# An attention block whose front part takes four score maxima and six projection products in turn, with the first rows of maxima written by VectorE

## The chip, the core and the metric

The kernel runs on one core of a Trainium2 chip. The engines that matter are TensorE (PE in the profile, its weight loads PEld), VectorE (DVE), ScalarE (ACT), GpSimd (POOL) and SyncE (SP), which issues nearly all the transfers. Each engine and each issuing queue works through its own list of instructions in the order in which the program gave them; between engines there are only semaphores. The metric is the device time of one execution in microseconds (us), median over the runs. Lower is better.

## The reference

One transformer block, 2048 rows of 512 numbers, float32. A modulation vector (six parts of 512) comes from a small product with `w_mod`. The first half is attention with 32 query heads of 16 numbers and one shared head of keys and values; the second half an MLP of width 1376.

```python
x = A_x
mod = (_silu(c) @ w_mod).reshape(c.shape[0], 6, 1, -1)
sa, ca, ga, sb, cb, gb = (mod[:, i] for i in range(6))
h = _layernorm(x) * (1 + ca) + sa
q = (h @ wq) in 32 heads of 16;  k = h @ wk;  v = h @ wv
p = softmax(q k^T / 4);  o = p v
x = x + ga * (o @ wo)
h = _layernorm(x) * (1 + cb) + sb
x = x + gb * (gelu(h @ w1 + b1) @ w2 + b2)
```

The softmax needs, for each of 32 x 2048 query rows, the largest of its 2048 scores before the exponentials.

## The kernel before

**Units.** The attention is cut into 64 units: 8 blocks of 256 query rows, each with 8 groups of four heads. For one unit the program does two things, far apart in time. First the maxima: 32 products `m` of 128 query rows against 512 keys (indices j, t, kc, s: s is one of two halves of the array's rows, so that an s=0 and an s=1 product run beside each other), each followed by one VectorE reduction over 512 scores (`Max.step`, L512 and L517). Then the exponentials: 8 steps, each with four products `e` (L617), four ScalarE exponentials (L621) and the products `acc` of the exponentials with the values (L638). The maxima run ahead of the exponentials by a lead that the loop holds with a table, `lead[u]`: `LEAD_0` counts groups of four maxima beyond unit 1 at the start, `LEAD` the same from unit 8 on, with a straight line between. `mp.done` is the number of maxima issued; in every pair of steps the loop issues as many as bring it to the goal.

**Placing the maxima.** When the 32 reductions of a unit are in, `put_max` reduces them over kc (`mm`), transposes the result (`turned`), copies it in four pieces into one row per score column (`mt`), splits it into a high part `mh` and a rest `ml`, and sends both by DMA into rows 48 and 49 of each half of the unit's query tile `qst`. The matching rows of the keys hold -1, so the products `e` come out with the maximum already taken off. No `e` of a unit can start before its four sends have landed. In the running loop the copies and the split are GpSimd's (L560, L133, L140) and the sends SyncE's (L555); they are asked for by `later(n, ...)`, n quarter-iterations after the reductions are complete, which fixes their place in each engine's list. Of unit 0 two of the four sends are issued by ScalarE.

**The front part.** Before the loop, an explicit list `SLOTS` interleaves the maxima of units 0 and 1 with the rest of the preparation: `"keys b"` is a group of three products of the key and value projection of row block b (twelve in all, `kps`), after the fourth group two ScalarE copies write the keys (`kv_out`, L401) and one the values (L402); `"low b"` is a VectorE subtraction that writes the low part of the keys (L407), `"k b"` its ScalarE copy; `"heads b"` a transposition group with modulation; `"q 1"` three products of the second query projection; `"v b"` a transposition of the values; `"rows"` a quarter of the late modulation rows (`modl`, L297); `"wq g"` the split of a weight block; `"load"` the six loads of unit 2's query tile (`load_q`, L483). A number in a slot is a count of maxima. `FIRST_MAX` says in which order: all of unit 0's are done after 48. The `m` products use a ring of three PSUM banks (tag `m`); the banks `e0` to `e2` (`ebank()`) serve the transpositions in the front and the products `e` in the loop.

**Products that nobody reads.** `keep_warm(n)` issues n full products whose result is unread, in four places, the last just ahead of the loop (`WARM[3]`).

**SyncE's list in the loop.** The same queue carries the loads of the next query tiles (`load_q`: six transfers, and two of `dz` from unit 4 on) and, in the first units, the sends of the query projections (`dq`), the loads and stores of the weights being prepared (`w1f`, `dw`), and for a short while the late modulation rows (`drm`, `ga`, `gb`, `sb`, `cb`).

Of the kernel before, what the change touches and what calls it, by code (L numbers as in the profile page):

```python
# [22 lines left out]
LEAD_0 = 6  # L23
FIRST_MAX = ((0, 0), (1, 0), (0, 1), (1, 1), (0, 2), (0, 3), (1, 2), (1, 3))
SLOTS = ((2, "keys 1", "keys 1"), (2, "keys 1", "keys 1"), (2, "low 1", "heads 2"), (2, "heads 2", "k 1"), (1, "warm"), (1, "heads 2"), (2, "heads 2", "v 0"),
# [19 lines left out]
WARM = (4, 16, 2, 5)  # L45
# [4 lines left out]
def raw(ap):  # L50
    return ap.bitcast(F32)
# [3 lines left out]
def adaln_mqa_mlp(  # L55
# [230 lines left out]
    def keep_warm(n, **place):  # L286

        for k in range(n):
            if k == 0 or not place:
                ps = psum.tile([P, BQ], F32, name=f"idle{len(idles)}", **(place or dict(tag="m", bufs=3)))  # L290
                idles.append(ps)
            nc.tensor.matmul(ps, wkH[:, 0, :], wkH.rearrange("p k n -> p (k n)"), start=True, stop=True)
# [98 lines left out]
    def kv_products(b):  # L391
        hH, hL = hts[b]
        kps[b] = psum.tile([P, BQ], F32, name=f"kps{b}", tag="x" if b == 3 else "v")
        return mm3(kps[b], [(wkH[:, k, :], wkL[:, k, :], hH[:, k, :], hL[:, k, :]) for k in range(KD)], 3)

    def kv_out(b):
        ps = kps[b]
        cols = slice(b * BQ, (b + 1) * BQ)
        vt = pro.tile([P, BQ], F32, name=f"vt{b}", tag="vt", bufs=2)
        for r in range(2):  # L400
            nc.scalar.copy(ks[64 * r:64 * r + 48, cols], ps[64 * r:64 * r + 48, :])  # L401
        nc.scalar.copy(vt[32:64, :], ps[32:64, :])  # L402
        vts[b] = vt

    def low_k(b):
        cols = slice(b * BQ, (b + 1) * BQ)
        nc.vector.tensor_tensor(out=ks[32:48, cols], in0=kps.pop(b)[32:48, :], in1=raw(ks[32:48, cols]), op=ALU.subtract)  # L407
# [128 lines left out]
    def put_max(u, mx):  # L536
# [13 lines left out]
        def send():  # L550
            for s in range(2):
                for r, src in ((48, mh), (49, ml)):
                    dst = qst[64 * s + r:64 * s + r + 1].rearrange("p j (t n) -> p (j t) n", n=P)
                    ring = nc.scalar if u == 0 and s else nc.sync
                    ring.dma_start(out=raw(dst), in_=raw(src[2 * T * s:2 * T * (s + 1), :].unsqueeze(1)))  # L555
            placed.add(u)
# [7 lines left out]
        def reduce():  # L564
            nc.vector.tensor_reduce(out=mm[:, :4 * T], in_=mx, axis=AX.X, op=ALU.max)
# [672 lines left out]

    def chunk(n):
# [5 lines left out]
    def k_products(b):  # L1245
        for _ in kv_products(b):
            pass
# [84 lines left out]
    run(keys(0))  # L1332
    low_k(0)
# [19 lines left out]
    for n, *names in SLOTS:  # L1353
        chunk(n)
        for name in names:
            next(work[name])
# [53 lines left out]
    keep_warm(WARM[3], tag="e2", bufs=1)  # L1410
# [172 lines left out]
```

## Time and profile before

| what | value |
|---|---|
| runs | 1558.17, 1556.62, 1556.4 us; median 1556.62 |
| the profiled execution's own time | 1555.99 us |
| its span, first to last instruction | 1554.1 us |
| granted TensorE clock | 1.00 throughout |
| busy: PE, DVE, ACT, POOL | 99%, 90%, 79%, 44% of the span |
| first `m` of the front part | 31.84 us |
| first `e` of the loop | 75.14 us |
| first `acc` of the loop | 78.88 us |

A busy PE is not PE at its peak: its instructions are pipelined and their ends are modelled, so two rows that follow each other are compared by their starts. A row such as "48.68 5.27 DVE ... x8" is eight instructions merged, from their first start to their last end. What stands in brackets is the idle time of the engine ahead of the row and who ended it.

### The profile page before, as it was taken

Reading aid. Unit: us, or ns where it says so; the run is one execution under the profiler, and the core shown is the slowest. Engines: PE = TensorE matmul, PEld = TensorE weight load, DVE = VectorE, ACT = ScalarE, POOL = GpSimd, SP = SyncE. Lnnn points to the kernel's source line nnn. Section 1 sums busy time; section 2 is a strip of 40 time slices with the busy share of each in tenths; the row PEclk is TensorE's granted clock in tenths of the full one; section 3 lists DMA queues with packets and bytes.
Section 4 is the critical chain, followed back from the end, with each engine's and each line's share of the span. In section 5 each row is a group of like instructions: output and inputs, shape, how many; then the busy total and the mean of one; then the engine's idle time right before and its main releaser. Section 6 shows DMA issues by size and latency. Waiting matters only on the chain.

```text
span 1554.1 us, 41556 instructions
## 1 busy us (share of the span) xinstructions
PE 1537.9 (99%) x16405; PEld 954.4 (61%) x16405; DVE 1398.3 (90%) x2488; ACT 1230.4 (79%) x2401; POOL 683.7 (44%) x1206
## 2 busy tenths in 40 slices
PE   7999999999999999999999999999999999999999
PEld 4455555567655665557655676556655676566658
DVE  7999999999999999999999999999999999999814
ACT  5577778788877887788877888788877888778874
POOL 5535432867422571246521563235711574046511
PEclk9999999999999999999999999999999999999999
DMA  7226412413030220303112120302212230203141
GB/s 240 102 89 199 151 57 81 130 51 97 18 105 26 72 68 28 103 19 109 33 51 79 56 87 16 111 26 88 68 30 73 60 101 25 87 28 99 48 150 48
DMA packets 84215, 120.85 MB, mean 78 GB/s; under 512 B 21342, under 2 KB 57438, under 8 KB 83764
## 3 DMA queue, kind: packets, MB, share of 16 engines
q1 hardware_dynamic: 84004, 118.18, 23.7%
q8 instruction: 130, 2.13, 0.6%
q14 instruction: 65, 0.53, 0.1%
q10 hardware_dynamic: 16, 0.00, 0.0%
HBM read 90.87 MB, written 26.74 MB: 76 GB/s over the span
## 4 chain that ended last, share of the span: by engine, by line
PE 86%; DVE 8%; issue 3%; POOL 2%; DMA 1%; ACT 0%; SPq 0%; POOLq 0%; DVEq 0%
PE acc L638 29%; PE m L512 23%; PE e L617 16%; PE w1ps L198 8%; DVE mx L517 6%; PE w2ps L198 2%; PE w2ps L188 2%; DMA xt<-in_A_x_dram 1%; PE w1ps L188 1%; PE wops L198 1%; PE tp L198 1%; PE qps L198 1%; PE kps L165 1%; DVE st L823 0%; DVE x L816 0%
## 5 line engine op out<-in xcount | busy, mean ns | idle before, releaser
L517 DVE TENSOR_REDUCE mx<-m 128x1 f32<-128x512 f32 x2048 | 1270.6, 682 | 86.6 <-PE m L512 65.1
L621 ACT ACTIVATE p<-e 128x512 f32<-128x512 f32 x2048 | 1098.8, 598 | 255.1 <-PE e L617 112.0
L512 PE MATMUL m<-ks,qst 64*128 64x512 f32 x2048 | 836.7, 429 | 2.0 <-DVE mx L517 0.6
L617 PE MATMUL e<-qst,ks 64*128 64x512 f32 x2048 | 740.2, 412 | 0.0
L638 PE MATMUL acc<-p,va 128*32 128x256 f32 x8192 | 548.0, 385 | 0.0
L512 PEld LDWEIGHTS m<-ks,qst 64*128 64x128 f32 x2048 | 368.2, 184 | 205.1 <-DVE mx L517 173.5
L617 PEld LDWEIGHTS e<-qst,ks 64*128 64x128 f32 x2048 | 359.6, 184 | 89.3 <-ACT p L621 62.5
L638 PEld LDWEIGHTS acc<-p,va 128*32 128x32 f32 x8192 | 214.0, 109 | 213.9 <-issue 110.9
L198 PE MATMUL w1ps<-h2H,w1t 64*128 64x256 f32 x1232 | 235.5, 287 | 0.0
L560 POOL TENSOR_SCALAR mt<-turned 8x32 f32<-8x32 f32 x256 | 53.1, 208 | 399.9 <-DVE turned L566 387.9
L198 PEld LDWEIGHTS w1ps<-h2H,w1t 64*128 64x128 f32 x1232 | 186.0, 185 | 28.9 <-DVE mx L517 14.8
L198 PE MATMUL w1ps<-h2L,w1t 64*128 64x256 f32 x616 | 169.3, 275 | 0.0
L198 PE MATMUL w2ps<-w2H,gH 64*128 64x512 f32 x274 | 120.3, 439 | 0.0
L198 PEld LDWEIGHTS w1ps<-h2L,w1t 64*128 64x128 f32 x616 | 114.1, 185 | 0.0
L198 PE MATMUL w2ps<-w2L,gH 64*128 64x512 f32 x274 | 107.5, 392 | 0.0
L198 PE MATMUL w2ps<-w2H,gL 64*128 64x512 f32 x274 | 106.9, 390 | 0.0
L975 POOL TENSOR_SCALAR tt<-tt 128x256 f32<-128x256 f32 x77 | 31.0, 402 | 131.5 <-ACT tt L974 96.5
L140 POOL TENSOR_TENSOR gL<-z,gH 128x256 fp32r<-128x256 f32 x77 | 57.0, 741 | 6.4
L976 POOL TENSOR_TENSOR tt<-tt,z 128x256 f32<-128x256 f32 x77 | 56.7, 736 | 6.4
L986 POOL TENSOR_TENSOR z<-tt,z 128x256 f32<-128x256 f32 x77 | 56.4, 732 | 6.0
L985 POOL TENSOR_TENSOR tt<-tt,z 128x256 f32<-128x256 f32 x77 | 56.5, 733 | 0.0
L198 PEld LDWEIGHTS w2ps<-w2H,gH 64*128 64x128 f32 x274 | 50.4, 184 | 6.7 <-DVE ot L1038 2.5
(193 smaller groups left out, 1503.5 us busy)
## 6 DMA issues: line engine op xcount, KB each, us to landing
w1t<-dw SPq DMA_DIRECT2D x82, 512.0 KB
qst<-dq SPq DMA_DIRECT2D x384, 32.0 KB
do<-oc SPq DMA_DIRECT2D x62, 128.0 KB
dw<-w1s SPq DMA_DIRECT2D x11, 512.0 KB
xt<-in_A_x_dram SPq DMA_DIRECT2D x4, 1024.0 KB
dq<-qH SPq DMA_DIRECT2D x16, 256.0 KB
dq<-qL SPq DMA_DIRECT2D x16, 256.0 KB
x<-in_A_x_dram SPq DMA_DIRECT2D x8, 512.0 KB
```

The lines of the kernel that those rows point to most:

```text
L140: eng_l.tensor_tensor(out=dst_l, in0=src, in1=raw(dst_h), op=ALU.subtract)
L188: nc.tensor.matmul(ps, a, b_, start=first_, stop=last_)
L198: ins = nc.tensor.matmul(ps, a[rows], b_[rows], start=first_ and s == 0, stop=last_ and s == 1)
L512: nc.tensor.matmul(m, qsts[u][rows, j, t * P:(t + 1) * P], ks[rows, kc * 512:(kc + 1) * 512], start=True, stop=True)
L517: nc.vector.tensor_reduce(out=self.mx[u][:, i, kc:kc + 1], in_=m, axis=AX.X, op=ALU.max)
L560: nc.gpsimd.tensor_scalar(out=mt[:, g:g + 32], in0=turned[g:g + 4 * T, :], scalar1=1.0, scalar2=0.0, op0=ALU.mult, op1=ALU.add)
L617: nc.tensor.matmul(e, ks[rows, kt * P:(kt + 1) * P], rhs, start=True, stop=True)
L621: ins = nc.scalar.activation(dst, e, AF.Exp, scale=0.25)
L638: ins = nc.tensor.matmul(accs[u][32 * cidx:32 * cidx + 32, :], va[:, kt, :], rhs, start=kt == 0, stop=kt == NKT - 1)
L976: nc.gpsimd.tensor_tensor(out=tt, in0=tt, in1=z, op=ALU.mult)
L985: nc.gpsimd.tensor_tensor(out=tt, in0=tt, in1=z, op=ALU.mult)
L986: nc.gpsimd.tensor_tensor(out=z, in0=tt, in1=z, op=ALU.add)
```

## The change

Five things, all in the front part or at its seam with the loop.

1. From the second block of keys on, a slot holds four maxima and two projection groups (six products) where it held two and one. In these slots (`WIDE`, up to the last but two) every second `m` takes one of the banks `e0` to `e2`, so that six banks carry maxima and not three.
2. The copy of the values out of the projection's bank (`keep_v`) is taken out of `kv_out` and put behind the copy of the low keys; the subtraction `low b` stands between two maxima.
3. Unit 0's maxima are placed by VectorE at once (`place_first`): four copies, one cast, one subtraction on VectorE, and two transfers, both by SyncE, each for both halves of the array. Before they were GpSimd's six operations and four transfers, two of them ScalarE's.
4. `LEAD_0` is 5: the loop starts with 52 maxima issued, not 56. The last slots hold two groups of two maxima between the four groups of late rows.
5. `WARM[3]` is 4: four unread products ahead of the loop, not five, from other data and into the bank of tag `v`.

```diff
-LEAD_0 = 6
+LEAD_0 = 5
...
-         (0, "v 2"), (2, "q 1"), (2, "q 1"), (2, "q 1"),
-         (2, "q 1", "rows"), (2, "v 3", "wq 2"), (2, "rows"), (2, "rows"), (2, "rows", "wq 3", "load"))
+         (4, "keys 2", "keys 2"), (4, "keys 2", "keys 2"), (2, "low 2", 2, "k 2", "keys 3", "keys 3", "v 1", "wq 1"), (4, "keys 3", "keys 3"),
+         (2, "low 3", 2, "k 3", "v 2", "q 1", "q 1"), (4, "q 1", "v 3", "q 1", "wq 2"), (4, "wq 3", "rows"),
+         (2, "rows"), (2, "rows"), ("rows", "load"))
+WIDE = 11
...
-WARM = (4, 16, 2, 5)
+WARM = (4, 16, 2, 4)
...
-            nc.tensor.matmul(ps, wkH[:, 0, :], wkH.rearrange("p k n -> p (k n)"), start=True, stop=True)
+            nc.tensor.matmul(ps, src[:, :P], src, start=True, stop=True)
...
         for r in range(2):
             nc.scalar.copy(ks[64 * r:64 * r + 48, cols], ps[64 * r:64 * r + 48, :])
-        nc.scalar.copy(vt[32:64, :], ps[32:64, :])
...
+    def keep_v(b):
+        vts[b] = pro.tile([P, BQ], F32, name=f"vt{b}", tag="vt", bufs=2)
+        nc.scalar.copy(vts[b][32:64, :], kps[b][32:64, :])
...
         nc.scalar.copy(ks[96:112, cols], raw(ks[32:48, cols]))
+        if b:
+            keep_v(b)
...
-                    ring = nc.scalar if u == 0 and s else nc.sync
-                    ring.dma_start(out=raw(dst), in_=raw(src[2 * T * s:2 * T * (s + 1), :].unsqueeze(1)))
+                    nc.sync.dma_start(out=raw(dst), in_=raw(src[2 * T * s:2 * T * (s + 1), :].unsqueeze(1)))
+            placed.add(u)
+
+        def place_first():
+            for g in range(0, P, 32):
+                nc.vector.tensor_copy(out=mt[:, g:g + 32], in_=turned[g:g + 4 * T, :])
+
+            def send_row(r, src):
+                dst = qst[r:r + 65:64].rearrange("p j (t n) -> p (j t) n", n=P)
+                nc.sync.dma_start(out=raw(dst), in_=raw(src.unsqueeze(1)))
+
+            split(mh, ml, mt, nc.vector, nc.vector, lambda: send_row(48, mh))
+            send_row(49, ml)
...
+            if u == 0:
+                place_first()
+                return
...
-            mp.step(mp.done % 2)
+            mp.step(mp.done % 2, **(ebank() if wide[0] and mp.done % 2 else {}))
...
-    keep_warm(WARM[3], tag="e2", bufs=1)
+    keep_warm(WARM[3], bigH[:, 0, 0, :], tag="v")
```

The order of the instructions shows three places. The first is TensorE's list where the second block's keys are projected (`kps`, three products to a group; `m_j_t_kc_s` are maxima, `qst_157` and `qst_158` the query tiles of units 0 and 1). Before:

```order
L165 MATMUL kps_646<-bigH,wkH 128x512
L165 MATMUL kps_646<-bigH,wkL 128x512
L165 MATMUL kps_646<-bigL,wkH 128x512
L512 MATMUL m_1_0_1_0_650<-ks,qst_157 128x512
L512 MATMUL m_1_0_1_1_653<-ks,qst_157 128x512
L165 MATMUL kps_646<-bigH,wkH 128x512
```

After:

```order
L517 MATMUL m_1_0_1_0_646<-ks,qst_157 128x512
L517 MATMUL m_1_0_1_1_649<-ks,qst_157 128x512
L517 MATMUL m_1_1_1_0_652<-ks,qst_157 128x512
L517 MATMUL m_1_1_1_1_655<-ks,qst_157 128x512
L166 MATMUL kps_658<-bigH,wkH 128x512
L166 MATMUL kps_658<-bigH,wkL 128x512
L166 MATMUL kps_658<-bigL,wkH 128x512
L166 MATMUL kps_658<-bigH,wkH 128x512
L166 MATMUL kps_658<-bigH,wkL 128x512
L166 MATMUL kps_658<-bigL,wkH 128x512
L517 MATMUL m_0_0_1_0_665<-ks,qst_158 128x512
```

Four maxima now stand ahead of the first group, and the array changes between half rows (`m`) and full rows (`kps`) half as often. The second place is VectorE's list where unit 0's maxima are complete. After:

```order
L522 TENSOR_REDUCE mx_482<-m_1_1_3_1_812 128x1
L581 TENSOR_REDUCE mm_192<-mx_482 128x8
L582 STREAM_TRANSPOSE turned_815<-mm_192 128x32
L564 COPY mt_818<-turned_815 8x32 x4
L138 CAST mh_819<-mt_818 8x128
L141 TENSOR_TENSOR ml_820<-mt_818,mh_819 8x128
L522 TENSOR_REDUCE mx_544<-m_0_0_2_0_840 128x1
```

Six operations have come in between the transposition and the next maximum, which stood side by side before. The third place is SyncE's list in the loop, in unit 3, where unit 4's maxima are sent (`mh`, `ml` into `qst_157`) and unit 6's query tile is loaded (`qst_159`). Before:

```order
L1120 DMA cb_69<-drm 128x4x1
L1178 DMA dw_104<-w1s_1971 128x1024
L555 DMA qst_157<-mh_2054 1x4x128
L555 DMA qst_157<-ml_2055 1x4x128
L555 DMA qst_157<-mh_2054 1x4x128
L555 DMA qst_157<-ml_2055 1x4x128
L483 DMA qst_159<-dq_3_90 16x2x256 x3
L485 DMA qst_159<-dz 2x512
L483 DMA qst_159<-dq_3_90 16x2x256 x3
L485 DMA qst_159<-dz 2x512
L1178 DMA dw_104<-w1s_2072 128x1024
```

After:

```order
L1139 DMA cb_69<-drm 128x4x1
L1197 DMA dw_104<-w1s_1962 128x1024
L1197 DMA dw_104<-w1s_2059 128x1024
L488 DMA qst_159<-dq_3_90 16x2x256 x3
L490 DMA qst_159<-dz 2x512
L488 DMA qst_159<-dq_3_90 16x2x256 x3
L490 DMA qst_159<-dz 2x512
L559 DMA qst_157<-mh_2115 1x4x128
L559 DMA qst_157<-ml_2116 1x4x128
L559 DMA qst_157<-mh_2115 1x4x128
L559 DMA qst_157<-ml_2116 1x4x128
```

The four sends have moved behind one store and eight loads. The same move, behind `load_q`, holds for units 1 to 6, since with the shorter lead their maxima are complete in the second pair of steps of the unit before and not in the first; `mm` and what follows it stand one pair of steps later in every list. The extra four maxima of the loop stand in two pairs of steps with five and five in place of four and four: at the start of units 2 and 6.

More of the change, by code (lines that the diff above doesn't have):

```diff
@@ L284, in adaln_mqa_mlp, with keep_warm @@
     idles = []
-    def keep_warm(n, **place):
+    def keep_warm(n, src=None, **place):
+        src = wkH.rearrange("p k n -> p (k n)") if src is None else src
         for k in range(n):
@@ L1237, in adaln_mqa_mlp @@
     mp = Max()
+    wide = [False]
     def chunk(n):
         for _ in range(n):
-            mp.step(mp.done % 2)
+            mp.step(mp.done % 2, **(ebank() if wide[0] and mp.done % 2 else {}))
     act, dve, pool = nc.scalar, nc.vector, nc.gpsimd
-    def k_products(b):
-        for _ in kv_products(b):
-            pass
     draining[0] = True
@@ L1332, in adaln_mqa_mlp @@
     run(keys(0))
+    keep_v(0)
     low_k(0)
@@ L1352, in adaln_mqa_mlp @@
             "wq 1": one(prep_wq, 1), "wq 2": one(prep_wq, 2), "wq 3": one(prep_wq, 3)}
[L1353 to L1356, printed above, removed]
+    for i, slot in enumerate(SLOTS):
+        wide[0] = WIDE <= i < len(SLOTS) - 2
+        for part in slot:
+            if isinstance(part, int):
+                chunk(part)
+            else:
+                next(work[part])
     assert 0 in placed and len(mods_late) == KD
```

4 lines of the change are left out of this document (1 added, 3 removed), and 3 rows, old and new, of the table SLOTS.

## Prediction, made before the run

> **What bounds the kernel now.** I read the page's chain first, then the windows by stage, then the timelines of the engines at the places that the change touches.
>
> ```profile
> PE 86%; DVE 8%; issue 3%; POOL 2%; DMA 1%; ACT 0%; SPq 0%; POOLq 0%; DVEq 0%
> 47.27:65.51 18.24, 17.96 (x71) 9.23 (x69) 17.05 (x28) 8.55 (x16) 8.46 (x9) 1.00 0.01 2
> 78.88:250.00 171.12, 171.05 (x1794) 99.71 (x1794) 158.65 (x272) 133.12 (x252) 73.18 (x113) 1.00 0.37 118
> ```
>
> The last two rows are windows: length, then busy time of PE, PEld, DVE, ACT and POOL, granted clock, DMA share. The loop is TensorE's: it never idles, and whatever makes it wait there is not won back. The stage of the projections in the front (47 to 65 us) has VectorE busy for 17.05 of 18.24 us, so it can give up about one microsecond to better packing before VectorE itself is full. I compare with this execution, 1555.99 us, 0.63 under the median.
>
> **The front.** Rows of TensorE, VectorE and ScalarE:
>
> ```profile
> 48.58 0.51 PE L165 MATMUL kps<-bigH,wkH 128*128 128x512 f32 x1
> 48.92 0.39 PE L165 MATMUL kps<-bigH,wkL 128*128 128x512 f32 x1
> 49.15 0.40 PE L165 MATMUL kps<-bigL,wkH 128*128 128x512 f32 x1
> 49.47 0.50 PE L512 MATMUL m<-ks,qst 64*128 64x512 f32 x2
> 49.90 0.51 PE L165 MATMUL kps<-bigH,wkH 128*128 128x512 f32 x1
> 45.70 2.47 DVE L517 TENSOR_REDUCE mx<-m 128x1 f32<-128x512 f32 x4
> 48.68 5.27 DVE L517 TENSOR_REDUCE mx<-m 128x1 f32<-128x512 f32 x8 [0.51 <-PE m L512]
> 54.04 0.68 DVE L407 TENSOR_TENSOR ks<-kps,ks 16x512 fp32r<-16x512 f32 x1
> 67.05 2.48 DVE L517 TENSOR_REDUCE mx<-m 128x1 f32<-128x512 f32 x4 [1.05 <-PE m L512]
> 75.91 7.27 DVE L517 TENSOR_REDUCE mx<-m 128x1 f32<-128x512 f32 x12 [0.85 <-PE m L512]
> 47.48 0.78 ACT L386 ACTIVATE h<-tp,sa,ca 128x512 f32<-128x512 f32 x1 [0.46 <-POOL bigL L140]
> ```
>
> Three products and a pair of maxima take 49.90 - 48.58 = 1.32 us of TensorE, though a product follows another after 0.23: the two changes of shape cost the rest. Two such periods are 2.64. With six products and two pairs, half the changes go: 0.34 + 4 x 0.23 + 0.32 for the products, 0.43 + 0.23 for the maxima, 2.24 us. VectorE, saturated, takes 7.27/12 = 0.606 a reduction, 2.42 for four. So VectorE becomes the bound, 0.22 us better for four maxima, and six banks let it stay fed while a subtraction waits.
>
> From the end of the reductions at 45.70 + 2.47 = 48.17 to unit 0's last one, at 67.05 + 2.48 = 69.53, VectorE has 28 reductions (28 x 0.606 = 17.0) and two subtractions (with their gaps 1.4): 18.4 of 21.4 us. I keep gaps of 0.7: at the start, because the new second bank waits for ScalarE to empty it (47.48 + 0.78 = 48.26), and before the last four. Unit 0's last reduction then ends at 48.17 + 18.4 + 0.7 = 67.3, 2.2 earlier. Bounds: 66.6 with no gap, 69.5 with all of the present ones.
>
> What follows it:
>
> ```profile
> 69.56 0.19 DVE L565 TENSOR_REDUCE mm<-mx 128x8 f32<-128x32 f32 x1
> 32.57 0.37 DVE L210 BATCH_NORM_AGGREGATE mv<-st 128x2 f32<-128x6 f32 x4
> 71.50 0.69 SPq L555 DMA_DIRECT2D qst<-mh  x1
> 72.29 0.61 SPq L555 DMA_DIRECT2D qst<-ml  x1
> 72.96 0.59 ACTq L555 DMA_DIRECT2D qst<-ml  x1
> 23.71 0.34 SPq L424 DMA_DIRECT2D dq<-qH  x1
> 25.72 8.80 SPq L483 DMA_DIRECT2D qst<-dq  x12
> 69.63 1.07 PE L297 MATMUL modl<-wml,csb 128*32 128x512 f32 x8
> 70.63 0.49 PE L512 MATMUL m<-ks,qst 64*128 64x512 f32 x2
> 71.05 1.07 PE L297 MATMUL modl<-wml,csb 128*32 128x512 f32 x8
> 73.75 1.47 PE L292 MATMUL idle<-wkH 128*128 128x512 f32 x5
> 75.14 0.49 PE L617 MATMUL e<-qst,ks 64*128 64x512 f32 x2
> 75.29 0.59 ACT L1364 COPY modl_sb<-modl 128x512 f32<-128x512 f32 x1 [0.96 <-ACT wqH L342]
> ```
>
> The data: the first send goes out 1.94 us after `mm` starts, the last, ScalarE's, at 72.96, and `e` starts at 75.14, so a send lands within 2.18 us of its issue; the first load of a query tile, which waits for a send issued at 23.71, goes out 2.01 after it. I take 2.0. After the change: `mm` and transposition 0.43, four copies about 0.5 (four small aggregates took 0.37), the cast 0.23, two issues on SyncE 0.8 apart, landing 2.0: 67.3 + 0.43 + 0.5 + 0.23 + 0.8 + 2.0 = 71.3. The Trainium skill speaks against many small VectorE operations ("VectorE: DVE Perf Modes", section "The TRN2 errata": each instruction whose source is in SBUF pays a fixed extra time, some 150 cycles at 0.96 GHz as measured there); by it the four copies would take 4 x 0.19 = 0.76 and not 0.5, and the loop would start 0.3 later; the row of four aggregates, at 0.09 apiece, does not bear it out for operations in a row.
>
> TensorE: with six banks it runs up to four reductions ahead (4 x 0.606), and a reduction starts about 0.4 after its product, so unit 0's last pair is issued some 2.8 us ahead of its last reduction's end, at 64.5 (an estimate); then 0.43, four groups of late rows and two pairs of maxima (1.42 for a group with its pair, 1.0 without), four unread products in place of five (1.39 x 4/5): 64.5 + 0.43 + 2 x 1.42 + 2 x 1.0 + 1.2 = 71.0. Both paths meet; the loop starts at 71.3 instead of 75.14, 3.8 earlier. Bounds: 70.3 (no gaps) and 73.3 (all gaps kept). ScalarE's copy of the late rows, which today ends at 75.88, a quarter of a microsecond behind the first `e`, comes out ahead of it: 0.1 more. The moved value copy lies beside VectorE's reductions; the cover gone, it would cost 0.58. The unread products keep a clock that is granted at 1.00 in every window.
>
> **The four maxima given to the loop.** They stand in four steps with five maxima.
>
> ```profile
> 116.04 1.07 PE L638 MATMUL acc<-p,va 128*32 128x256 f32 x16
> 118.88 1.07 PE L638 MATMUL acc<-p,va 128*32 128x256 f32 x16
> 113.08 0.69 DVE L463 COPY q<-qps 128x512 f32<-128x512 f32 x1
> 117.58 2.49 DVE L517 TENSOR_REDUCE mx<-m 128x1 f32<-128x512 f32 x4 [0.23 <-PE m L512]
> ```
>
> A step is 2.84 us. A fifth maximum has no partner in the other half of the array: at least 0.23 of TensorE each, 0.9 in all. At most VectorE's time counts whole, 4 x 0.606 = 2.4. VectorE idles 0.23 in a step by the last row, and in the first of the two pairs it has a projection's copy as well. I take 1.2, nearer TensorE's price, since a copy of 0.69 is absorbed today without a visible delay.
>
> **The sends of units 1 to 6 come later.** They move by a pair of steps, 5.7 us. For unit 1 and unit 4:
>
> ```profile
> 87.09 0.57 SPq L555 DMA_DIRECT2D qst<-ml  x1
> 97.44 0.39 PE L617 MATMUL e<-qst,ks 64*128 64x512 f32 x1
> 158.35 0.50 SPq L1178 DMA_DIRECT2D dw<-w1s  x1
> 161.41 0.57 SPq L555 DMA_DIRECT2D qst<-ml  x1
> 162.03 1.87 SPq L483 DMA_DIRECT2D qst<-dq  x3
> 166.27 0.43 SPq L485 DMA_DIRECT2D qst<-dz  x1
> 165.87 0.39 PE L617 MATMUL e<-qst,ks 64*128 64x512 f32 x1
> 152.52 0.38 SPq L1169 DMA_DIRECT2D w1f<-in_B_w_dram  x1
> 157.09 0.62 POOL L133 TENSOR_SCALAR w1s<-w1f 128x512 fp32r<-128x512 f32 x1 [2.72 <-DMA w1f<-in_B_w_dram]
> ```
>
> Unit 1: last send at 87.09, landed at 89.1, wanted at 97.44: 8.3 us to spare, 2.6 after the move. Units 2, 3, 5 and 6 read alike, and the eight loads that now stand ahead of their sends wait for nothing late, so they go out while SyncE is idle: no cost. Unit 4 is the exception. There SyncE is already late (the store at 158.35 stands behind weights and modulation rows, none of which moves), the last send goes out at 161.41 and only 2.5 us are left. Now one more store (0.5) and eight loads (162.03 to 166.70, 4.7) stand ahead of the sends: the last goes out at about 161.41 + 5.1 = 166.5, or 166.2 with the shorter issues of other units, lands at 168.2, and the first `e` of unit 4, wanted at 165.87, holds TensorE for 2.3 us. GpSimd isn't later: it has `ml` by 161. Bounds: 0, if the queue runs ahead of this reckoning or a landing takes no time; 4.9, if a landing takes the 4.57 us of the weight load that went out at 152.52 and was used at 157.09.
>
> **Sum.** -3.8 (loop start) - 0.1 (first exponential) + 1.2 (five maxima) + 2.3 (unit 4) = -0.4 us. On the profiled execution 1555.6; on the median 1556.62 - 0.4 = 1556.2 us.
>
> **Rivals.**
> - *The sends of unit 4 land in time* (nothing at 165.87): -2.7, 1553.9 us. For it: SyncE's lateness there hangs on transfers whose landing varies. Against it: all the rows ahead of it are unmoved.
> - *VectorE's gaps stay*, as the keys' subtraction waits for ScalarE and ScalarE for the bank: the loop starts at 73.3, 2.0 later than I say, +1.6, 1558.2. For it: the 18.24 us stage has 1.2 idle only.
> - *Slower: the sends miss their units.* All of units 1 to 6 have 2.6 us left. Beyond a landing of 4.6 us each unit waits; at the 5.6 that would be a microsecond in five units and 5.9 in unit 4, so 3.6 more there, -0.4 + 5 + 3.6 = +8.2, 1564.8 us. Against it: landings of about 2.0 in the rows.
> - *The front doesn't change* because the wide banks are held by the transpositions: then the loop starts earlier only by what four maxima fewer (two pairs, 0.9) and one unread product fewer (0.3) take: -1.2 + 1.2 + 2.3 = +2.3, 1558.9 us.
>
> **Chances.** The sum as worked out 0.47; unit 4 in time 0.30; gaps stay 0.11; sends miss 0.08; front unchanged 0.04. 0.2% is 3.1 us, about what a measurement tells from no change: faster means under 1553.5, slower over 1559.7. The case of unit 4 in time straddles the lower bound, since the front's term can reach -4.8: half of it, and a little of the first, gives 0.18 faster. Sends that miss, and tails of the first, third and fifth, give 0.14 slower; 0.68 between. The likeliest case alone spans 1554.6 to 1557.8. The range for all, 1552.9 to 1559.6: below, unit 4 in time with one microsecond more in the front; above, gaps kept with VectorE's full price (1.2 more).
>
> **What would show it.** Right: unit 0's last reduction near 67.3, the first `e` near 71.3; `acc` starts 2.84 apart but for four steps of about 3.1; an idle TensorE of about 2.3 us ahead of one `e` at the start of unit 4, with SyncE's last `ml` of that unit behind its loads. Wrong: no such idle, idle ahead of the first `e` of other units, or VectorE idle for more than a microsecond between 48 and 67 us.

## The result, and the profile after

The changed kernel takes 1564.18 us (median of six runs, 1562.32 to 1566.62); the kernel before took 1556.71 beside it. The ratio is 1.0048, with a 95% interval of 1.0035 to 1.0061. The profiled execution took 1563.32 us, its span 1561.5, with a granted clock of 0.998. One run of the last experiment took 2811.1 us and is left out of its numbers.

Where the 7.4 us of span arise can be read from one row per unit, ScalarE's copy of the finished `acc`, which ends a unit. From ScalarE's timeline of the kernel before, units 0, 2, 3, 6 and 63:

```profile
100.08 0.37 ACT L650 COPY oc<-acc 128x256 f32<-128x256 f32 x1
...
145.68 0.37 ACT L650 COPY oc<-acc 128x256 f32<-128x256 f32 x1
...
168.52 0.37 ACT L650 COPY oc<-acc 128x256 f32<-128x256 f32 x1
...
235.57 0.37 ACT L650 COPY oc<-acc 128x256 f32<-128x256 f32 x1 [0.22 <-PE acc L638]
...
1507.49 0.37 ACT L650 COPY oc<-acc 128x256 f32<-128x256 f32 x1 [0.73 <-PE acc L638]
```

And of the changed kernel, the same units:

```profile
98.85 0.37 ACT L669 COPY oc<-acc 128x256 f32<-128x256 f32 x1
...
145.91 0.37 ACT L669 COPY oc<-acc 128x256 f32<-128x256 f32 x1
...
173.37 0.37 ACT L669 COPY oc<-acc 128x256 f32<-128x256 f32 x1 [0.81 <-PE acc L657]
...
241.61 0.37 ACT L669 COPY oc<-acc 128x256 f32<-128x256 f32 x1 [0.22 <-PE acc L657]
...
1514.40 0.37 ACT L669 COPY oc<-acc 128x256 f32<-128x256 f32 x1 [0.73 <-PE acc L657]
```

Unit 0 ends 1.23 us ahead of the kernel before; unit 2 is 0.23 behind it; unit 3, whose copy stands behind unit 4's first step, 4.85 behind; unit 6, 6.04 behind. From there to the last unit it grows to 6.91 only, in small steps. So a gain of 1.2 at the start is spent twice over in the first seven units: 1.46 over units 1 and 2, 4.62 between units 2 and 3, 1.19 between units 3 and 6.

Four windows of the changed kernel: the last ten microseconds ahead of where the loop started before, the loop's first 171 us (the prediction shows this one for the kernel before), and 3.4 us and 3.9 us behind two waits of TensorE (length, busy PE, PEld, DVE, ACT, POOL, granted clock, DMA share):

```profile
65.51:75.14 9.63, 7.63 (x52) 2.84 (x48) 8.65 (x17) 3.76 (x9) 4.40 (x7) 0.95 0.17 62
78.88:250.00 171.12, 168.03 (x1718) 96.86 (x1720) 155.30 (x264) 128.04 (x241) 73.19 (x113) 0.99 0.35 115
73.71:77.12 3.41, 3.41 (x15) 2.31 (x16) 2.82 (x6) 2.87 (x6) 0.00 (x0) 0.57 0.19 48
169.07:173.00 3.93, 3.93 (x28) 2.18 (x28) 2.08 (x3) 2.22 (x4) 0.00 (x0) 0.59 0.65 253
```

TensorE now idles 3.1 us within the loop's first 171 (it idled 0.07), and 2.0 ahead of it. And behind each of the two gaps stands a stretch in which the granted clock is about half, where it was 1.00 throughout.

The start of the loop, from the timelines of VectorE, GpSimd, SyncE, TensorE and ScalarE of the changed kernel:

```profile
50.87 3.68 DVE L522 TENSOR_REDUCE mx<-m 128x1 f32<-128x512 f32 x6 [0.42 <-PE m L517]
...
59.18 1.29 DVE L522 TENSOR_REDUCE mx<-m 128x1 f32<-128x512 f32 x2 [0.20 <-PE m L517]
...
65.69 2.48 DVE L522 TENSOR_REDUCE mx<-m 128x1 f32<-128x512 f32 x4 [0.80 <-PE m L517]
68.67 2.35 DVE L564 COPY mt<-turned 8x32 f32<-8x32 f32 x4
71.06 0.22 DVE L138 CAST mh<-mt 8x128 fp32r<-8x128 f32 x1
67.88 1.44 POOL L345 TENSOR_TENSOR wqL<-wqf,wqH 128x256 fp32r<-128x256 f32 x2
69.26 0.15 POOL L100 MEMSET pad<- 128x64 f32 x1
69.37 1.44 POOL L345 TENSOR_TENSOR wqL<-wqf,wqH 128x256 fp32r<-128x256 f32 x2
72.07 0.53 SPq L568 DMA_DIRECT2D qst<-ml  x1
73.71 0.50 PE L636 MATMUL e<-qst,ks 64*128 64x512 f32 x2 [2.00 <-DMA qst<-ml]
70.70 0.59 ACT L1385 COPY modl_sb<-modl 128x512 f32<-128x512 f32 x1 [2.88 <-POOL wqL L345]
```

Unit 0's last reduction ends at 68.17, 1.36 sooner; VectorE idles for 0.42, 0.20 and 0.80 us on the way there. Then the four copies take 2.35 us, the last row goes out at 72.07, and `e` starts 1.64 later, with TensorE idle for 2.00.

Unit 4, from the timelines of SyncE and TensorE of the changed kernel:

```profile
159.22 2.70 SPq L488 DMA_DIRECT2D qst<-dq  x3
...
165.27 0.65 SPq L559 DMA_DIRECT2D qst<-mh  x1
...
167.33 0.57 SPq L559 DMA_DIRECT2D qst<-ml  x1
169.07 0.46 PE L636 MATMUL e<-qst,ks 64*128 64x512 f32 x1 [2.82 <-DMA qst<-ml]
...
171.37 1.93 PE L657 MATMUL acc<-p,va 128*32 128x256 f32 x16
```

The four sends stand behind the eight loads, the last goes out at 167.33, and TensorE waits 2.82 us for it. The sixteen products `acc` that follow take 1.93 us instead of 1.07.

### The profile page after: what moved, and what is told of

Read it like the earlier page. It is cut to its first block, busy times and chain, and to the rows that moved or that the text cites. A ratio compares the mean times of both kernels' runs of the same rounds, so it can differ in the third digit from the quotient of the medians.

```text
span 1561.5 us, 41548 instructions
## 1 busy us (share of the span) xinstructions
PE 1540.9 (99%) x16404; PEld 956.2 (61%) x16404; DVE 1401.2 (90%) x2494; ACT 1230.8 (79%) x2401; POOL 682.3 (44%) x1200
## 4 chain that ended last, share of the span: by engine, by line
PE 84%; DVE 8%; issue 3%; POOL 2%; DMA 2%; SPq 1%; ACT 1%; POOLq 0%; DVEq 0%
PE acc L657 29%; PE m L517 23%; PE e L636 16%; PE w1ps L199 8%; DVE mx L522 6%; PE w2ps L199 2%; PE w2ps L189 2%; PE w1ps L189 1%; DMA xt<-in_A_x_dram 1%; PE wops L199 1%; PE tp L199 1%; PE qps L199 1%; POOL xt L375 1%; DVE st L842 0%; PE kps L166 0%
```

## The experiments

A diff against the changed kernel unless it says otherwise. Offsets are the end of a unit against the kernel before, read as above. In some executions the whole front part is 0.6 to 0.8 us late from its first `m` on (32.5 for 31.9 us), whatever the kernel; where a profile is one of those, the text says so.

**The lead back at 56.**

```
-LEAD_0 = 5
+LEAD_0 = 6
```

> The changed kernel with the lead back at 56 maxima (LEAD_0 = 6), wide slots and first rows by VectorE kept. Theory A (the loss is made in the loop by the shorter lead: unit 4's rows leave the queue too late, 4.6 us, and two pairs of steps with five maxima, 2.3 us): both vanish, the first exponential's product comes at 73.7 to 75.5 us, the time is 1555.5 to 1558.5 us, and acc of unit 4 starts without a step in its offset. Theory B (the four maxima are only moved, and cost the same before the loop as in it; the rest of the loss is the wide front): the loop starts 2.4 us later than in the changed kernel and the time is 1561 us or more.

1560.25 us, ratio 1.0020 (1.0010 to 1.0031). The offset is +2.95 at unit 0, +2.99 at unit 4 and +2.98 at unit 6: what the loop lost is gone altogether. But the start is 4.2 us later than in the changed kernel (0.6 of it is the late front part of this execution). From the timelines of VectorE and TensorE of this run:

```profile
72.16 4.86 DVE L522 TENSOR_REDUCE mx<-m 128x1 f32<-128x512 f32 x8
...
72.89 0.50 PE L517 MATMUL m<-ks,qst 64*128 64x512 f32 x1 [1.67 <-DVE mx L522]
74.08 1.69 PE L517 MATMUL m<-ks,qst 64*128 64x512 f32 x3 [0.70 <-DVE mx L522]
75.70 1.97 PE L294 MATMUL idle<-bigH 128*128 128x512 f32 x4
77.60 0.80 PE L636 MATMUL e<-qst,ks 64*128 64x512 f32 x2
```

With eight maxima ahead of the loop, three banks and a VectorE that first places unit 0's rows, TensorE waits for banks, then works at half clock (1.97 us for four unread products that take 1.19 at full clock), and `e` comes at 77.60. Theory A holds for the loop, neither theory for the start: with the longer lead, VectorE's placement makes the maxima wait.

**The sends ahead of the loads.**

```
-MAX_WAIT = (1, 4)
+MAX_WAIT = (1, 2)
```

> The changed kernel with the rows of maxima sent two quarter steps sooner (MAX_WAIT = (1, 2)), which puts each unit's sends ahead of the next unit's loads in SP's queue; the lead stays at 52. Theory A: only unit 4's wait goes, with its half-clock stretch: 4.6 us less than the changed kernel, 1559.6 us; the two steps with five maxima still cost 2.3 us. Theory C (the sends are late because the maxima themselves are late, not because of the queue): the wait at unit 4 stays at 2 us or more, and the time is 1562 us or more.

1560.63 us (1.0024; 1.0014 to 1.0033), 3.6 less than the changed kernel. The profiled execution took 1558.03 us at a clock of 0.999, the fastest of the ten; six of the others had 0.998. Unit 4 from the windows of this run:

```profile
165.00:190.00 25.00, 25.00 (x268) 14.94 (x267) 23.09 (x40) 19.33 (x37) 10.75 (x16) 1.00 0.34 116
```

TensorE is busy throughout and the clock is full. The offsets are -1.13 at unit 0, +0.34 at unit 2, +0.35 at unit 3, +1.53 at unit 6: the step of 4.62 is gone, those of 1.47 and 1.18 stay. The maxima of unit 4 are in time; its sends were late by their place in SyncE's list. And the two stretches with the five maxima cost 2.65 us without a wait at unit 4.

**More unread products ahead of the loop.**

```
-WARM = (4, 16, 2, 4)
+WARM = (4, 16, 2, 10)
```

> The changed kernel with ten unread products before the loop instead of four: 3.0 us at 0.30 each from 70.5 us, so TensorE is busy until 73.5 us and the first product for an exponential still comes at 73.7. Theory A: the half-clock stretch at 74 to 77.5 us goes; the steps' offsets say that it costs 0.2 to 0.35 us there, so 1563.9 us. Theory D (a half-clock stretch costs half its length whatever is running): 1.7 us less, 1562.5 us. If the stretch stays at half clock, it isn't the idle time that brings it.

1563.08 us (1.0043; 1.0028 to 1.0058). The stretch behind the first `e` is gone as either theory said, but in the profiled execution another one stands at 49 to 52.5 us, behind 0.73 us of idle time just ahead of the wide slots, and delays the front by 1.4, so the run doesn't price the first stretch. It prices the second one: here TensorE waits at unit 4 as before, and no stretch at half clock follows.

```profile
165.00:190.00 25.00, 22.37 (x238) 13.07 (x236) 20.85 (x36) 17.55 (x33) 7.84 (x14) 1.00 0.32 109
```

The step between units 2 and 3 is 2.85 us instead of 4.62, and 2.63 of it is the wait, for 2.82 of 4.62. What stands beyond the wait is 0.22 without the stretch and 1.80 with it, so the stretch at half clock cost about 1.6 us there, nearly half of its 3.4.

**Unit 0's rows by GpSimd again.**

```
         def reduce():
...
-            if u == 0:
-                place_first()
-                return
...
-                    nc.sync.dma_start(out=raw(dst), in_=...)
+                    ring = nc.scalar if u == 0 and s else nc.sync
+                    ring.dma_start(out=raw(dst), in_=...)
```

> The changed kernel with unit 0's rows placed as before: GpSimd gathers and splits, four transfers of one row on two queues. Theory A (four copies on VectorE at 0.59 apiece take what the shorter way was to give): from the end of unit 0's last reduction (68.2 us) to the first product for an exponential 5.6 us as in the kernel before, so the same start within 0.3 us, VectorE free 3 us sooner, and 1563.5 to 1564.5 us. The prediction's terms (copies 0.5 in all, two issues, 4.0 us in all) would make GpSimd's way 1.5 us slower: 1565.7 us.

1562.45 us (1.0040; 1.0025 to 1.0055), 1.1 less than the least expected. The start is the same: last reduction ends at 68.12, the first `e` comes at 73.69, unit 0 at -1.01. VectorE's placement gained nothing on GpSimd's six operations and four sends.

**The wide slots alone** (lead 56, unit 0's rows as before; the moved copy of the values and the four unread products come with them):

```
-LEAD_0 = 5
+LEAD_0 = 6
```

and the edit of the run before this.

> Only the wide slots and the unread products on other operands: lead 56, unit 0's rows by GpSimd and four transfers as before. Theory A: unit 0's last reduction 1.3 us sooner (68.2 for 69.5), the copy chain and the landing as before, so unit 0 ends 1.0 us ahead of the kernel before, with nothing lost later: 1555.6 us. Theory E (the wide slots let TensorE wait for VectorE ahead of the loop, and stretches at half clock follow): unit 0's lead of 1 us is lost in most executions, the granted clock of the runs falls to 0.999 or 0.998, and the median is 1556.6 us or above.

1557.09 us (1.0000; 0.9991 to 1.0010). The last reduction ends at 68.07, but unit 0 ends at +0.41. From TensorE's timeline and the windows:

```profile
74.51 0.56 PE L634 MATMUL e<-qst,ks 64*128 64x512 f32 x2 [1.18 <-DMA qst<-ml]
66.00:79.00 13.00, 11.54 (x66) 4.44 (x62) 11.03 (x21) 6.13 (x14) 5.96 (x13) 0.93 0.16 56
```

The rows are waited for, 1.18 us, and a stretch at half clock follows. Over ten runs the clock was 1.000 in four, 0.999 in four and 0.998 in two, and the four at 1.000 took 1555.0 to 1556.8, the others 1557.0 to 1558.5. Theory E, but what TensorE waits for is the rows and not VectorE.

**The shorter lead alone**, in the kernel before:

```
-LEAD_0 = 6
+LEAD_0 = 5
...
-... (2, "rows"), (2, "rows"), (2, "rows", "wq 3", "load"))
+... (2, "rows"), (0, "rows"), (0, "rows", "wq 3", "load"))
```

> The kernel before with a lead of 52 maxima (LEAD_0 = 5, four maxima less in its last two slots). Theory A: the start doesn't move (GpSimd's gathering and the landing gate the first product), then units 1 and 2 lose 1.46 us, unit 4's late sends 2.9 us of waiting and up to 1.8 of half clock, units 5 and 6 1.2 us: 1562.2 to 1564.0 us. If the loss in the loop needs the wide front, 1557 to 1558 us.

1562.99 us (1.0041; 1.0029 to 1.0054). The offsets: +1.31, +1.81, +2.44, +5.35, +5.35, +5.97, +6.58 at units 0 to 6, +6.93 at the last. From unit 0 to unit 6 that is 5.3: 1.1 for the first five maxima, 2.91 for unit 4's wait without half clock, 1.2 for the second five maxima. The start is 0.27 later for `e`, and a stretch at half clock behind an idle TensorE of 1.15 us makes 1.31 of it. The loss in the loop needs nothing of the rest of the change.

**VectorE's placement alone**, in the kernel before: `place_first` as in the changed kernel, called where unit 0's maxima are complete, and nothing else.

```
+            if u == 0:
+                place_first()
+                return
             later(MAX_WAIT[0], gather)
```

> The kernel before with unit 0's rows placed by VectorE and two transfers, and nothing else. Theory A: VectorE spends 3.0 us on copies and split while eight maxima wait for banks, so the eighth is issued at 76.2 and the first product for an exponential comes at 77.5 to 78.2 for 75.14: 1559 to 1560.5 us. The prediction's terms for it (0.5 for the copies, 1.5 us less from the reduction to the first product): 1555 to 1556.5 us.

1561.51 us (1.0029; 1.0018 to 1.0040). The eighth maximum is issued at 75.43, the first `e` at 78.58, 3.4 late, with a clock of 0.81 from 66 to 79 us: theory A, and 1 us more by the half clock. Here the four copies take 1.53 us, not 2.35.

**The wide slots with ScalarE placing the rows:**

```
-LEAD_0 = 5
+LEAD_0 = 6
...
         def place_first():
             for g in range(0, P, 32):
-                nc.vector.tensor_copy(out=mt[:, g:g + 32], in_=turned[g:g + 4 * T, :])
+                nc.scalar.copy(mt[:, g:g + 32], turned[g:g + 4 * T, :])
...
-            split(mh, ml, mt, nc.vector, nc.vector, lambda: send_row(48, mh))
+            split(mh, ml, mt, nc.scalar, nc.gpsimd, lambda: send_row(48, mh))
```

> The wide slots with lead 56, and unit 0's rows copied and cast by ScalarE, the low part by GpSimd, two transfers. If a copy of 8x32 costs ScalarE about 0.2 us, the first row is ready at 69.7, the second at 70.4, and the first product comes at 72.3 to 72.8, bound by VectorE's eight maxima: unit 0 ends 2.0 us or more ahead of the kernel before, 1554.5 us. If copies that read one group of partitions and write another cost 0.59 on any engine: unit 0 1.0 us ahead, 1555.6 us, as the wide slots alone.

1555.31 us (0.9989; 0.9980 to 0.9998), granted clock 1.000 in all ten runs; unit 0 ends at -1.72. From the timelines of ScalarE and TensorE:

```profile
68.77 0.90 ACT L564 COPY mt<-turned 8x32 f32<-8x32 f32 x4 [1.49 <-DVE turned L582]
...
73.43 0.50 PE L636 MATMUL e<-qst,ks 64*128 64x512 f32 x2
```

Four copies in 0.90 us on an engine that was idle, 0.22 apiece as the first theory said. TensorE reaches `e` without a wait, from its maxima and its unread products, 0.6 us later than expected, so the gain is a little smaller.

**Four copies by themselves.** Behind the last output of that kernel, on VectorE (the last group on ScalarE), from a constant into a tile no longer used:

```
+    for g in range(0, P, 32):
+        nc.vector.tensor_copy(out=prb[:8, g:g + 32], in_=ident[g:g + 8, 0:32])
+    for g in range(0, P, 32):
+        nc.vector.tensor_copy(out=prb[:8, P + g:P + g + 32], in_=ident[0:8, g:g + 32])
+    ... (as multiply and add; 32x32; on ScalarE)
```

> The wide slots with ScalarE's placement, and behind the last output five groups of four small copies of a constant: on VectorE 8x32 from partitions 0, 32, 64, 96 to partition 0; the same from partitions 0 to 7 alone; the first group as a multiply and add; 32x32 from the four groups of partitions; and the first group on ScalarE. If what makes VectorE's copies in the changed kernel long is the start at another group of 32 partitions, the first, third and fourth group take 0.6 to 0.7 us a copy and the second 0.1 to 0.2. If it is the plain copy of a small tile, the second takes 0.6 as well and the third not. If it was the data or other work at that place, all take 0.2 or less. ScalarE: 0.22 in each case.

From VectorE's timeline of this run:

```profile
1554.28 0.71 DVE L1577 COPY p<-ident 8x32 f32<-8x32 f32 x4
1555.00 0.42 DVE L1579 COPY p<-ident 8x32 f32<-8x32 f32 x4
1555.35 0.71 DVE L1581 TENSOR_SCALAR p<-ident 8x32 f32<-8x32 f32 x4
1556.08 0.72 DVE L1583 COPY p<-ident 32x32 f32<-32x32 f32 x4
```

0.16 to 0.17 us a copy in every form. A start at another group of partitions costs only the overlap, 0.71 for four instead of 0.42. So neither the form nor the partitions made the copies long in the changed kernel.

**The wide slots alone with eight unread products:**

```
-WARM = (4, 16, 2, 4)
+WARM = (4, 16, 2, 8)
```

on the wide slots alone.

> The wide slots alone (lead 56, unit 0's rows by GpSimd) with eight unread products before the loop instead of four, so that TensorE isn't idle for 1.18 us before the first product for an exponential; the product itself still comes at 74.5. If that idle time brings the half-clock stretch behind it: granted clock 1.000 in nearly all runs, unit 0 ends 0.5 to 0.9 us ahead of the kernel before instead of 0.4 behind, and the median falls by 1 to 1.5 us to 1555.6 to 1556.1. If the stretch comes from somewhere else in the front part: no change, 1557.1.

1556.49 us (0.9996; 0.9987 to 1.0005). Clock 1.000 in nine of ten runs, unit 0 at -0.08 in an execution whose front part was 0.8 late. With four unread products the clock was 1.000 in four of ten, so it is the idle time that brings the stretch. The gain over four, 0.6, is about half of what was expected, and the two intervals overlap.

**ScalarE's placement in the kernel before:** the edit to `place_first` above, in the kernel with VectorE's placement alone.

> The kernel before with unit 0's rows copied and cast by ScalarE and two transfers, narrow slots. The chain over the rows is 1.1 us shorter, but TensorE itself is busy until 74.8 behind VectorE's eight maxima: the first product at 75.0 for 75.14, 1556.2 to 1556.6 us. If the rows' chain gates the start: 1 us less, 1555.5 us, and then the wide slots have no part in what the faster kernel gained.

1556.74 us (0.9999; 0.9990 to 1.0008). Nothing gained: the first `e` comes at 75.54 in an execution that is 0.65 late, straight behind the unread products. TensorE itself gates the start in the kernel before. The wide slots are needed for the gain.

**ScalarE's placement with two unread products:**

```
-WARM = (4, 16, 2, 4)
+WARM = (4, 16, 2, 2)
```

on the wide slots with ScalarE placing the rows.

> The wide slots with ScalarE's placement and two unread products instead of four: TensorE comes free at 73.0 instead of 73.43, and the rows land at 72.4 to 72.9. 0.4 us less than with four, 1554.9 us; if an idle time then arises ahead of the first product and brings a half-clock stretch, 1555.5 to 1557 us.

1554.72 us over eleven runs (0.9987; 0.9978 to 0.9996), the fastest of all. From the timelines of TensorE and VectorE:

```profile
72.93 0.50 PE L636 MATMUL e<-qst,ks 64*128 64x512 f32 x2
68.62 10.55 DVE L522 TENSOR_REDUCE mx<-m 128x1 f32<-128x512 f32 x17
```

No idle time ahead of `e`, and VectorE reduces from unit 0's last maximum into the loop without a gap, so VectorE seems to be what bounds the start now; that wasn't tried.

**GpSimd's pieces behind the placement.** `"wq 2"` and `"wq 3"` go to the end of the last slot, and the first of GpSimd's four subtractions waits for `ml`:

```
+            if g == 2 and j == 0:
+                wait_for(ins, first_split[0], "GpSimd is idle while VectorE copies")
```

> The changed kernel, with the four pieces of weights that GpSimd splits at 67.9 to 70.8 us (wqL) put behind VectorE's placement of unit 0's rows by a wait. Theory F (a copy on VectorE waits for whatever GpSimd instruction runs, as the two use the same port: three of the four copies end when a piece of GpSimd ends, 0.72 apiece): the four copies take 0.7 us in all instead of 2.35, and the first product for an exponential comes at 72.1 to 72.4 us. ScalarE's copy of the modulation rows, which waits for the last piece, comes 3 us later, so the first exponential gains less than the product. Theory G (the copies are long because they read what VectorE has just transposed): 2.35 us as before.

From the timelines of VectorE, GpSimd and TensorE of this run:

```profile
68.74 0.72 DVE L568 COPY mt<-turned 8x32 f32<-8x32 f32 x4
...
70.26 2.84 POOL L347 TENSOR_TENSOR wqL<-wqf,wqH 128x256 fp32r<-128x256 f32 x4 [2.17 <-DVE ml L576]
...
72.12 0.50 PE L642 MATMUL e<-qst,ks 64*128 64x512 f32 x2 [0.35 <-DMA qst<-ml]
```

0.72 us for the four copies, `e` at 72.12, unit 0 at -3.02 (ScalarE's copy of the modulation rows did not come later, against what was expected beside the theories). Theory F; the one run took 1560.27, since the losses in the loop stay.

**The four copies as maxima over one element.**

```
-                nc.vector.tensor_copy(out=mt[:, g:g + 32], in_=turned[g:g + 4 * T, :])
+                nc.vector.tensor_reduce(out=mt[:, g:g + 32], in_=turned[g:g + 4 * T, :].unsqueeze(2), axis=AX.X, op=ALU.max)
```

> The changed kernel with the four copies written as maxima over an axis of one element, VectorE and everything else as it is, GpSimd's pieces beside them. Theory F, if only the copying form takes the port that GpSimd uses: 0.7 us for the four, the first product at 72.1 to 72.4 for 73.71, idle time of TensorE 0.5 us instead of 2.0 and no half-clock stretch behind it; unit 0 ends 2.4 to 2.8 us ahead of the kernel before instead of 1.2, the loop's losses stay: 1561.5 to 1563 us. If any VectorE instruction waits for GpSimd there, or theory G holds: no change, 1564 us.

1560.79 us (1.0015; 0.9999 to 1.0031), in the profiled execution with a front part 0.65 late. From the timelines of VectorE and GpSimd:

```profile
69.33 0.74 DVE L564 TENSOR_REDUCE mt<-turned 8x32 f32<-8x32 f32 x4
70.10 0.75 DVE L138 CAST mh<-mt 8x128 fp32r<-8x128 f32 x1
70.89 0.73 DVE L141 TENSOR_TENSOR ml<-mt,mh 8x128 fp32r<-8x128 f32 x1
68.54 1.44 POOL L345 TENSOR_TENSOR wqL<-wqf,wqH 128x256 fp32r<-128x256 f32 x2
...
70.03 1.44 POOL L345 TENSOR_TENSOR wqL<-wqf,wqH 128x256 fp32r<-128x256 f32 x2
```

The four take 0.74 us beside a busy GpSimd. But the cast and the subtraction behind them, 0.22 and 0.28 in the changed kernel, now meet the same pieces and take 0.75 and 0.73. The wait has only moved on, to the next operations of a form that waits: `e` at 73.28, with 0.92 of the 2.0 us idle left and half clock behind it, and unit 0 ends only 0.96 ahead. Theory F for the copies; the start gained less than it said. The time is below the expected range all the same: in this profile no half clock follows unit 4's wait, and the step there is 2.88 us.

**The same with the sends ahead of the loads:**

```
-MAX_WAIT = (1, 4)
+MAX_WAIT = (1, 2)
```

> The last one with the sends two quarter steps sooner, so that of the losses only the two pairs of steps with five maxima are left. By the offsets of the units: -2.4 to -2.8 at unit 0, +1.46 over units 1 and 2, nothing at unit 4, +1.2 over units 5 and 6, so 0 to +0.3 at unit 8 and about 0.8 more to the end: 1556.5 to 1557.5 us. If the shorter start makes the rows of later units late again: a step at units 3 or 4 and 1558 us or more.

The median of nine runs is 1557.69 us (0.9998; 0.9979 to 1.0016). The profiled execution is one of the slower ones, 1559.34. Offsets: -0.84 at unit 0 (0.7 of late front in it; -2.4 to -2.8 was expected), +0.60 at unit 2, +0.58 at unit 3, +1.76 at unit 6, +2.95 at the last unit. Up to unit 6 the terms add up: a start ahead, 1.44 and 1.18 for the five maxima, nothing at unit 4. The other 1.2 us come in small steps over the rest. With the placement and the sends mended, the shorter lead pays back just what the front part gains.

## Why the prediction was wrong

It gave 1556.2 us with a range to 1559.6; the time is 1564.18. Every term had its mechanism, and nearly every one was too small a cost or too large a gain. Of its own signs, the idle time at unit 4 came; but so did two that it named as signs of being wrong, VectorE idle for 1.42 us between 48 and 67 us and TensorE idle ahead of the first `e` of another unit, unit 0. Step by step:

- **Unit 0's last reduction: 67.3 predicted, 68.17 measured.** The reductions are VectorE's bound, 0.61 apiece, as said. But I kept 0.7 us of VectorE's gaps, and 1.42 stayed (0.42 at 50.87, 0.20 at 59.18, 0.80 ahead of the last four). Within the bounds given; 0.9 of the gain is missing. The rival *VectorE's gaps stay* describes this.
- **From there to the first `e`: 4.0 predicted, 5.54 measured. The step that failed is "four copies about 0.5": they took 2.35.** Landing (1.64 for 2.0) and the issues (0.73 for 0.8) were a little better than taken. The cause is shown: alone, four such copies take 0.71 (the probe); with GpSimd's pieces moved away, 0.72; in another form, beside the pieces, 0.74. GpSimd's pieces are 0.74 long, and the first three copies took 0.77, 0.68 and 0.68: each ended 0.03 us after GpSimd finished an instruction (at 69.41 the short fill behind the second piece, at 70.11 and 70.80 the third and the fourth piece). The last copy, behind the pieces, took 0.17. In the kernel with only the placement changed, pieces covered two copies and the four took 1.53. I read the price of a copy from other VectorE rows and never looked at what GpSimd does at that moment, though its row there (two pieces at 68.22 before the change) was in the trace and the change put two more beside the copies. The rule of the Trainium skill that I weighed gave 0.76 for the four, which agrees with the 0.71 of the probe; the 0.09 apiece of the aggregates, by which I put it aside, does not hold for copies that start at different groups of partitions. But neither is the reason. The rule that bears is another: the Trainium skill, "SBUF — State Buffer", section "SBUF: two separate sides", says that VectorE in its two-port copying modes, or with two inputs in SBUF, and GpSimd take turns at one pair of ports, for a whole instruction at a time. This case's traces agree: copy, cast and subtraction waited for pieces of 0.74 us, the one-input maximum did not. That GpSimd's instructions make the copies long is shown by the runs; that ports are the reason is what the page says, and no run here shows the ports.
- **Loop start: -3.8 predicted, -1.43 for the first `e`, -1.23 at the end of unit 0.** The sum of the two points above; the half clock behind the first `e` takes the other 0.2. The first `e`, at 73.71, lies outside the bounds of 70.3 to 73.3. (By the prediction's own working four unread products are 1.1 us and not the 1.2 in its sum; they took 1.20.) That ScalarE's copy of the modulation rows goes out ahead was right (70.70).
- **Four steps with five maxima: 1.2 predicted, 2.65 measured** (sends ahead of the loads). I took it nearer TensorE's price since VectorE seemed to have a quarter of a microsecond in a step. Each such step is 0.46 to 0.59 longer, so VectorE's whole 0.61 counts; and 0.37 more falls in a step of unit 1. The shorter lead alone doesn't bring those 0.37, since the kernel before with that lead loses only 1.13 over units 1 and 2 and not 1.46; their cause stays open. My upper bound, 2.4, was VectorE's time for the four alone.
- **Unit 4's sends: 2.3 predicted; the wait is 2.82, and 1.80 came on top, about 1.6 of it by half clock.** The reading of SyncE's list was right in kind and nearly in time: the last send at 167.33 (166.2 to 166.5 said), landing 1.74 (2.0 said). Adding this term to the others was right too, though the prediction took the queue's times from the kernel before: SyncE's list moves with the loop, and the wait is 2.70, 2.82 and 2.66 in kernels whose unit 2 ends 1.55 ahead, 0.23 behind and 2.44 behind. That units 1, 2, 3, 5 and 6 wait for nothing was right too: the trace has two waits of `e` for `ml`, 2.0 and 2.8 us.
- **The clock.** The step "the unread products keep a clock that is granted at 1.00 in every window" failed. A window of the kernel before says nothing about a kernel with idle time in it, and I had forecast idle time myself, at unit 4, and priced it at its length. The step at unit 4 is 2.85 without a half-clock stretch and 4.62 with one. The six runs of the changed kernel at clocks of 0.999, 0.999, 0.998, 0.997, 0.996 and 0.996 took 1562.3, 1562.6, 1563.3, 1565.1, 1566.1 and 1566.6 us. In the profile, 0.998 is two stretches of 3.4 us; counted the same way, 0.996 is nearly four (an estimate).
- **The sum**, with what was measured: -1.2 (start) + 1.5 and 1.2 (five maxima) + 4.6 (unit 4) + 0.9 (from unit 6 to the last) + 0.5 behind the last unit = +7.5, against 7.4 of span and 7.5 of the medians. The 0.9 in small steps appear with other starts of the loop as well (0.9 with the lead back at 56, 0.6 with the sends ahead, 0.1 with the wide slots and eight unread products), and about 0.5 behind the last unit stand in eight other profiles, of faster and slower kernels; the cause of both wasn't tried and stays open. The range was too narrow because each bound was drawn for its own term: with all three slower bounds together (2.0 at the start, 1.2 for the maxima, 2.6 at unit 4) it would have reached 1562.0. And the clock, which depends on two of the terms, had no bound at all. Of the rivals, the slower one I gave 0.08 had nearly the right time (1564.8), by luck, as its mechanism is wrong: the landings were faster than I took them.

## What to carry to other kernels

Before pricing a small VectorE copy, cast or two-input operation, look at what GpSimd runs in the same microsecond: here each waited for GpSimd instructions of 0.74 us, and ScalarE did the same four copies in 0.90 untouched. An idle time of TensorE of a microsecond or more has to be priced with up to 1.6 us of half clock behind it, so a wait taken on can be dearer than its length, and a few unread products that cover it to its end are cheap. A lead cut at the start of a pipeline moves every later hand-over behind whatever stands next in the queues: reorder the queue with it, or keep the lead; with lead and queue untouched, the wide slots and ScalarE's placement beat both kernels (1554.72 us, 0.9987).

## What the runs showed that was not expected of the hardware

- VectorE's copies, casts and two-input subtractions wait for a running GpSimd instruction and a one-input reduction doesn't: 0.68 to 0.77 against 0.17 us for the same copy alone, 0.75 and 0.73 against 0.22 and 0.28 for the cast and the subtraction.
- TensorE's clock drops to half for 3.4 us behind idle times much shorter than that: behind 0.9, 1.15, 1.18 and 2.0 us ahead of the first `e`, and once behind 0.73 in the front part (in two other profiles the same idle time there brought none). With 0.35 us or less ahead of the first `e` none followed (six profiles), nor behind 0.61 in one. The Trainium skill, "TensorE: Matmul & The Clock Gate", section "Part 1: The HAM clock gate (the "warmup" mystery)", speaks of half clock after at least one idle window of some 3.4 us, in windows that run freely. The length of the stretch agrees with that, and so do the windows, as the next point shows; that a whole window must be idle does not.
- At unit 4, of the six kernels with a wait of 2.6 to 2.8 us, three show the stretch behind it and three don't, and the traces show which. In each trace the changes of the clock lie whole multiples of 3.41 us apart (74.20, 77.62, 169.78 and 173.19 in the changed kernel), so windows of that length can be laid through it. The one that holds the wait in the changed kernel, and the two that share it in the kernel with ten unread products:

```profile
166.36:169.78 3.42, 0.71 (x6) 0.72 (x8) 0.62 (x1) 0.21 (x1) 0.00 (x0) 1.00 0.28 106
169.78:173.19 3.41, 3.41 (x25) 1.49 (x22) 2.08 (x3) 2.02 (x4) 0.00 (x0) 0.50 0.53 208
...
165.04:168.45 3.41, 2.40 (x28) 1.02 (x24) 2.75 (x5) 1.98 (x4) 1.09 (x2) 1.00 0.12 33
168.45:171.87 3.42, 1.80 (x16) 1.35 (x20) 1.07 (x2) 1.20 (x3) 0.00 (x0) 1.00 0.63 243
```

  In the three kernels with the stretch, most of the wait lies in one window, where TensorE is busy for 0.71, 0.72 and 1.08 us, and half clock begins at that window's end. In the three without, a window's edge divides the wait, and no window has less than 1.73 us. Ahead of the loop busy time doesn't decide as cleanly (a window with 2.50 us brought a stretch, one with 2.20 did not), so what the clock goes by stays open.
- Where half clock falls on work that TensorE bounds, it costs about half its length: about 1.6 us of 3.4 at unit 4.
